# Output product with the weights as the stationary operand, and earlier due times behind the first top-k passes

## The chip, the cores and the metric

The kernel runs on one core of one Trainium2 chip. The metric is the device time of one execution in microseconds (us); the median of three runs of the kernel before is 1257.34 us (1255.83 to 1258.74). The engines are named as the profile names them: PE (TensorE matmuls), PEld (TensorE weight loads), DVE (VectorE), ACT (ScalarE), POOL (GpSimd), SP (the queue that issues the DMAs).

## What is computed

Attention that keeps the 32 largest scores of each row, then a gated feed-forward layer, then a second layer with a cosine. All in float32; 4 batches of 576 rows make 2304 tokens, 8 heads of 64 make 512 columns.

```python
scores = scale * np.matmul(q, k.transpose(0, 1, 3, 2))
kth = np.partition(scores, -top_k, axis=-1)[..., -top_k:-top_k + 1]
scores = np.where(scores >= kth, scores, -1000000000.0)
...
x = attention output as (2304, 512)
g = x @ w_gate
x = (silu(g) * (x @ w_val)) @ w_out      # 512 -> 1536 -> 512
h = x @ w_in                             # 512 -> 2048
out = (h * np.cos(h)) @ w_out2           # 2048 -> 512
```

## The kernel before

The 2304 tokens are 18 blocks of 128. `SIZES` puts them into ten chunks: two chunks of one block (c = 0 and 1, `TURNED`, c < `PLAIN`) and eight chunks of two blocks (c = 2 to 9). A chunk goes through four kinds of work.

**Attention** (`unit_proc`, `pair_proc`, `av_proc`, `x_proc`). A unit is one block and one head; there are 144. For each, PE makes the scores (L586 for c < 3, L593 later), ACT copies them out (L598), DVE runs four MAX8 (L623) and three MATCH_REPLACE8 (L626), and what follows the top-k passes is: POOL makes the bounds (L637, L641), ACT masks and exponentiates (L654, L665), PE transposes (L687) with ACT copying (L693), PE multiplies with V (L743), and POOL and ACT scale the rows by the sums (L754 to L824). For c < 2 the result is written by L807, later by L820 and L824.

**Gate and value product** (`turned_gemm_proc`, L989, for c < 2; `gemm_proc`, L899, later). For c >= 2 all operands are split into a high and a low part, so one product is three matmuls: high by high, high by low, low by high. There the weights are the stationary operand, 128 x 128, and 256 tokens move past them. The result G has the hidden columns in partitions and the tokens in the free dimension.

**Output product** (`wout_proc`, L1063; then `y_proc`). For each of the 12 groups f of 128 hidden columns and each of the two token blocks t, the stationary operand is the 128 x 128 slice of G and the 512 columns of the weights WO move: three matmuls of 512 columns. Each block has a PSUM bank of its own (`yt`, two banks). The sum stands with tokens in partitions, and the second layer needs it the other way round, so `y_proc` copies half a bank to SBUF (L1096, ACT), transposes it back into the bank in two 128 x 128 pieces (L1102, PE), copies it out again (L1107, ACT) and stores it to `y1` in DRAM (L1108, SP). The SBUF buffer `yo` is a single one (`r_yo = Ring(1)`), so the next half waits for the store.

**Second layer** (`h_proc`, L1279; `o_proc`, L1344), from some 850 us on; it reads `y1` back.

**Weight conversions.** The weights come in as 64-bit views and are brought into their form by `convert` (POOL L239 and L244, ACT L241 and L242) and split into high and low part (`w1_rest`, ACT L290, POOL and DVE L294). WO is loaded per chunk and f by `wo_proc` into two buffers.

**What sets the order.** Every step of work is yielded to a planner (`Plan`) with an engine, an estimated cost and a due time. The planner runs a model of the engines when the program is built: an engine that becomes free takes, of the steps that are ready in the model, the one that is due first. That fixes the order of the instructions in each engine's queue; on the chip an engine works through its queue in order. A unit's due time is 4.97 us times its number; what follows the top-k passes is due 0 to 15 us after it. The first conversions are due from -2.6 us on at steps of 3.1 us. `moe_due` gives the due times of a chunk's products.

Of the kernel before, what the change touches and what calls it, by code (L numbers as in the profile page):

```python
# [23 lines left out]
NTOK = B * S  # L24
# [137 lines left out]
def topk_attention_moe_moe(ctx: ExitStack, tc: tile.TileContext, qT, kT, vP, w1, wo1, w2, out):  # L162
# [53 lines left out]
    def due_unit(u):  # L216
        return u * PACE


# [346 lines left out]
    def unit_proc(u):  # L566
# [71 lines left out]

        end = yield "POOL", 0.175, bounds, due, True
        r_m.free(u, end, plan)  # L640
# [14 lines left out]

        end = yield "ACT", 0.68, keep, due + 6.0, True
        if h == 0:
# [9 lines left out]

        end = yield "ACT", 0.77, expo, due + 9.0, True
        ev_exp[u].set(end, plan)
# [4 lines left out]
    def group_proc(c, p, t, g, pt, made, done):  # L674
        u = unit_of[c, p, t, 1]
        due = due_unit(u) + 11.0 + g
        j0, j1 = GROUPS[g]
# [43 lines left out]
    def av_proc(c, p, g):  # L721
# [23 lines left out]

        due = due_unit(unit_of[c, p, t0 + n - 1, 1]) + 15.0
        end = yield "PE", 0.34 * len(segs) + 1.13 * n, attv, due, True
# [12 lines left out]
    def x_proc(c, p, g):  # L760
        t0, n = ATT[c][g]
        key = c, p, g
        due = due_unit(unit_of[c, p, t0 + n - 1, 1]) + 12.0
        yield ev_sum[key]
# [81 lines left out]
    GV0 = [sum(NF1 // 4 if turned else NF1 for turned in TURNED[:c]) for c in range(NCH)]  # L846
    ev_y1 = [Event() for _ in range(NTOK // 128)]
# [200 lines left out]

    def wout_proc(c):
        turned = TURNED[c]  # L1050
        for f in range(NF1):
            k = c * NF1 + f
            yield ev_g[c, f]
            yield ev_wo[c, f]

            def part(t, f=f, k=k):
                bank = yt[(FIRST[c] + t) % NYB]
                cs = slice(t * 128, t * 128 + 128)
                g = G[c, f // 2][:, f % 2] if turned else None
                terms = ((g, WO[k]),) if turned else [(G[c, f][m][:, cs], WO[k][:, a])  # L1060
                                                      for m, a in ((0, 0), (1, 0), (0, 1))]
                for n, (m, w) in enumerate(terms):
                    nc.tensor.matmul(bank, m, w, start=f == 0 and n == 0, stop=f == NF1 - 1 and n == len(terms) - 1)  # L1063

            for t in range(SIZES[c]):
                i = FIRST[c] + t
                if f == 0:
                    yield r_y[i % NYB].gate(i // NYB)
                end = yield "PE", 0.93 if turned else 0.7, lambda t=t, part=part: part(t), moe_due(c, f) + 5.0, False
                if f == NF1 - 1:  # L1070
                    plan.start(y_proc(c, i), end)
            if not turned:
                r_g.free(G0[c] + f, end, plan)
            elif f % 2 and f // 2 >= NG0:
# [5 lines left out]
        if turned:  # L1080
            r_x.free(2 + c, end, plan)

    def y_proc(c, i):
        due = moe_due(c, NF1)
        bank = yt[i % NYB]
        y4 = bank.rearrange("p (f n) -> p f n", f=KT)
        for half in range(2):
            ko = yo_count[0]
            yo_count[0] += 1
            yield r_yo.gate(ko)  # L1090
            y2 = y4[:, 2 * half:2 * half + 2]
# [14 lines left out]
            def store(y2=y2, half=half):  # L1106
                nc.scalar.activation(st["y"], y2, AF.Copy)  # L1107
                nc.sync.dma_start(y1[:, 2 * half:2 * half + 2, i * 128:i * 128 + 128], st["y"])  # L1108

            end = yield "ACT", 0.27, store, due, True  # L1110
            r_yo.free(ko, end + 2.5, plan)
        r_y[i % NYB].free(i // NYB, end, plan)
        ev_y1[i].set(end + 2.5, plan)

# [104 lines left out]
    def x2_proc(j):  # L1219
        yield ev_pb  # L1220
        pb = pools["pb"]
        for i in range(j * TPB, (j + 1) * TPB):
            yield ev_y1[i]
        due = b_due(j, 0) - (25.0 if j else 75.0)
# [23 lines left out]
    def h_proc(j, f):  # L1248
# [11 lines left out]
        if second:  # L1260
            yield r_y[i % 2].gate(NTOK // 128 // NYB)
        elif not third:
            yield ev_ph
# [128 lines left out]
    for c in range(NCH):  # L1392
        for f in range(NF1):
            if c:
                plan.start(wo_proc(c, f))
            if not TURNED[c]:
                plan.start(gemm_proc(c, f))
            elif f % 2:
                plan.start(turned_gemm_proc(c, f // 2))
        plan.start(wout_proc(c))  # L1400
    plan.start(pool_b_proc())
# [50 lines left out]
```

## Time and profile before

| | us |
|---|---|
| median of three runs | 1257.34 |
| the profiled execution | 1255.94 |
| its span, from the first instruction to the last | 1253.9 |
| PE busy in the span | 1200.3 (96%) |
| PEld busy | 1043.6 (83%) |
| DVE busy | 975.1 (78%) |
| ACT busy | 923.8 (74%) |
| POOL busy | 632.0 (50%) |

The page gives one execution. The span leaves 2.0 us of that execution's time outside, and the profiled execution is 1.4 us below the median. A share of the whole span is an average over the first layer with its attention and the second layer, so it has to be read stretch by stretch.

### The profile page before, as it was taken

The page shows a single profiled execution, that of the slowest core. Times are in us where ns is not written, and L with a number is a line of the kernel's source. Part 1 is how long each engine was busy: PE and PEld are TensorE (multiplying, and loading weights), DVE is VectorE, ACT ScalarE, POOL GpSimd, SP SyncE. Part 2 cuts the span into 40 slices and gives each one's busy share as a digit, 9 for nine tenths or more (in the row PEclk, how much of TensorE's full clock was granted, in tenths as well). Part 3 has the DMA queues.
Part 4 walks back from the last instruction along what each step waited for, and adds up shares of the span by engine and source line. Part 5 has one row for each costly group of instructions (what it writes and reads, how often), then busy time and mean ns, then how long its engine had stood idle before and what let it go on. Part 6 is the DMA issues. An engine that isn't in the chain of part 4 may idle for free.

```text
span 1253.9 us, 22487 instructions
## 1 busy us (share of the span) xinstructions
PE 1200.3 (96%) x7528; PEld 1043.6 (83%) x7528; DVE 975.1 (78%) x1938; ACT 923.8 (74%) x2081; POOL 632.0 (50%) x1082
## 2 busy tenths in 40 slices
PE   6799889999999999999999999999999999999998
PEld 3577657898888898988898988897999989898997
DVE  6999999999999999998999993447555555555553
ACT  4789999899888888888898876557565656565554
POOL 4898976776777776877776755533010101010000
PEclk9799989999999999999999999999999999999999
DMA  7555556665656655556555332871010101010000
GB/s 253 159 175 168 179 163 201 206 211 168 194 164 180 190 170 175 181 162 203 181 160 189 124 116 85 268 261 39 1 51 1 51 1 51 1 38 1 18 8 26
DMA packets 88547, 162.14 MB, mean 129 GB/s; under 512 B 17008, under 2 KB 44144, under 8 KB 88432
## 3 DMA queue, kind: packets, MB, share of 16 engines
q1 hardware_dynamic: 88272, 160.65, 40.4%
q8 instruction: 59, 0.97, 0.3%
q14 instruction: 56, 0.46, 0.1%
q10 hardware_dynamic: 160, 0.07, 0.0%
HBM read 133.41 MB, written 27.26 MB: 128 GB/s over the span
## 4 chain that ended last, share of the span: by engine, by line
PE 58%; DMA 8%; ACT 6%; POOL 3%; DVE 2%; issue 2%; SPq 0%; POOLq 0%; ACTq 0%
PE o L1344 16%; PE h L1279 15%; PE gv L899 10%; PE y L1063 7%; PE av L743 2%; PE sc L593 2%; DMA wo<-wo 2%; DMA kx<-in_kT 2%; PE tp L687 2%; PE gvl L899 2%; DMA y<-yo 1%; DMA w_raw<-in_w 1%; DMA qx<-in_qT 1%; ACT e L654 1%; POOL K L496 1%
## 5 line engine op out<-in xcount | busy, mean ns | idle before, releaser
L623 DVE MAX8 m<-w 128x8 f32<-128x576 f32 x432 | 311.0, 747 | 1.8
L899 PE MATMUL gv<-x,w 128*128 128x256 f32 x2016 | 283.7, 288 | 1.7 <-ACT hg L866 1.6
L899 PEld LDWEIGHTS gv<-x,w 128*128 128x128 f32 x2016 | 259.0, 190 | 8.6 <-ACT hg L866 2.8
L1279 PE MATMUL h<-x2h,w 128*128 128x384 f32 x768 | 214.5, 338 | 0.0
L626 DVE MATCH_REPLACE8 w<-m,w 128x576 f32<-128x576 f32 x288 | 213.3, 742 | 0.0
L1344 PE MATMUL o<-w,gh 128*128 128x512 f32 x576 | 195.8, 395 | 0.0
L1242 POOL TENSOR_TENSOR x2l<-x,x2h 128x384 fp32r<-128x384 f32 x24 | 25.8, 1075 | 262.1 <-ACT x2h L1231 262.1
L1063 PE MATMUL y<-wo,gh 128*128 128x512 f32 x400 | 148.5, 413 | 6.7 <-DMA wo<-wo 5.1
L1313 DVE TENSOR_TENSOR g<-r,h 128x384 f32<-128x384 f32 x96 | 53.1, 554 | 118.5 <-ACT r L1308 118.5
L1279 PEld LDWEIGHTS h<-x2h,w 128*128 128x128 f32 x768 | 140.6, 188 | 4.3
L1279 PE MATMUL h<-x2l,w 128*128 128x384 f32 x384 | 129.3, 337 | 0.0
L1306 ACT ACTIVATE r<-r 128x384 f32<-128x384 f32 x96 | 50.4, 525 | 103.9 <-DVE r L1303 103.9
L1344 PEld LDWEIGHTS o<-w,gh 128*128 128x128 f32 x576 | 108.1, 188 | 21.0
L654 ACT ACTIVATE e<-s,b 128x576 f32<-128x576 f32 x144 | 114.2, 794 | 8.2 <-POOL b L637 8.1
L623 DVE MAX8 m<-s 128x8 f32<-128x576 f32 x144 | 107.7, 748 | 15.9 <-ACT s L598 14.5
L665 ACT ACTIVATE e<-e,b 128x576 f32<-128x576 f32 x144 | 114.2, 793 | 2.8 <-POOL b L641 0.3
L1344 PE MATMUL o<-w,gl 128*128 128x512 f32 x288 | 113.6, 394 | 1.0 <-DVE gl L1327 1.0
L598 ACT ACTIVATE s<-sc 128x576 f32<-128x576 f32 x144 | 95.4, 662 | 21.6 <-PE sc L586 16.2
L626 DVE MATCH_REPLACE8 w<-m,s 128x576 f32<-128x576 f32 x144 | 106.9, 742 | 0.0
L693 ACT ACTIVATE pt<-tp 128x512 f32<-128x512 f32 (+1 forms) x216 | 101.9, 503 | 4.9 <-PE tp L687 3.3
L687 PE MATMUL tp<-ident,e 128*128 128x128 f32 x648 | 99.4, 277 | 5.9 <-ACT pt L693 3.3
L1327 DVE TENSOR_TENSOR gl<-g,gh 128x384 fp32r<-128x384 f32 x96 | 56.4, 588 | 58.0 <-ACT gh L1324 58.0
(106 smaller groups left out, 2489.6 us busy)
## 6 DMA issues: line engine op xcount, KB each, us to landing
wo<-wo SPq DMA_DIRECT2D x96, 512.0 KB, 3.7
w_raw<-in_w SPq DMA_DIRECT2D x32, 511.8 KB, 4.3
V<-in_vP SPq DMA_DIRECT2D x52, 256.0 KB, 3.0
w<-in_w SPq DMA_DIRECT2D x24, 511.5 KB, 5.5
kx<-in_kT SPq DMA_DIRECT2D x64, 144.0 KB, 3.1
wo<-wo SPq DMA_DIRECT2D x36, 256.0 KB, 2.9
w2d<-w_raw SPq DMA_DIRECT2D x32, 256.0 KB, 2.6
cvx<-w2d SPq DMA_DIRECT2D x32, 256.0 KB, 4.5
```

The source lines that it names most:

```text
L598: nc.scalar.activation(st["s"], sc[:, :, :HALF], AF.Copy)
L623: nc.vector.max(out=st["m"][:, 8 * i:8 * i + 8], in_=st["w"] if i else st["s"])
L626: nc.vector.match_replace(out=st["w"], in_to_replace=st["m"][:, 8 * i:8 * i + 8], in_values=st["w"] if i else st["s"], imm_value=LOWEST)
L654: nc.scalar.activation(st["e"], st["s"], AF.Prelu, bias=st["b"][:, 1:2], scale=SCALE, alpha=STEEP)
L665: nc.scalar.activation(st["e"], st["e"], AF.Exp, bias=st["b"][:, 2:3], scale=1.0, accum_out=smT[c, p, g][:, j:j + 1])
L687: nc.tensor.transpose(st["ps"][:, j - j0], e[:, j * 128:j * 128 + 128], ident)
L693: nc.scalar.activation(pt[:, j0:j1], st["ps"][:, :j1 - j0], AF.Copy)
L899: nc.tensor.matmul(gv[g], W1[f, kk // 2][:, a, g, kk % 2], m, start=kk == 0 and i == 0, stop=kk == KT - 1 and i == 2)
L1063: nc.tensor.matmul(bank, m, w, start=f == 0 and n == 0, stop=f == NF1 - 1 and n == len(terms) - 1)
L1279: nc.tensor.matmul(st["h"], w[:, a, kk * 128:kk * 128 + 128], m[:, kk], start=kk == 0 and n == 0, stop=kk == KT - 1 and n == 2)
L1327: end = yield "DVE", 0.46, lambda: nc.vector.tensor_sub(GT[j, f][1], st["g"], GT[j, f][0]), due, True
L1344: nc.tensor.matmul(o[t], a[:, cs], W2[f, 1][:, m], start=f == 0 and n == 0, stop=f == NF2 - 1 and n == 2)
```

## The change

For c >= 2 the output product takes WO as the stationary operand and lets the 256 tokens of G move. The sum then comes out with the 512 output columns in partitions, in four pieces d of 128 columns by 256 tokens, two pieces to a bank, and needs no transposing: a piece is copied out by one ACT instruction and stored. Chunks 0 and 1 keep the old form, as `turned_wout_proc`. For chunk 8 (`late`) the four copies go to four buffers of their own in the pool that opens when attention has ended. Beside that, for c < 2, the due times of what follows the top-k passes are 12 us earlier (`soon`), and the planned cost of a score step changes from 0.98 to 1.25 us for c < 3 and from 0.575 to 0.58 later.

```diff
+    y1p = [x.rearrange("p (a b) -> p a b", a=2) for x in yt]
+    def soon(c):
+        return 12.0 if c < PLAIN else 0.0
-        end = yield "PE", 0.575 * len(segs) if c >= RAWC else 0.98, qk, due - SC_LEAD, True
+        end = yield "PE", 0.58 * len(segs) if c >= RAWC else 1.25, qk, due - SC_LEAD, True
-        end = yield "POOL", 0.175, bounds, due, True
+        end = yield "POOL", 0.175, bounds, due - soon(c), True
-        end = yield "ACT", 0.68, keep, due + 6.0, True
+        end = yield "ACT", 0.68, keep, due + 6.0 - soon(c), True
-        end = yield "ACT", 0.77, expo, due + 9.0, True
+        end = yield "ACT", 0.77, expo, due + 9.0 - soon(c), True
...
+    def wout_proc(c):
+        t0 = FIRST[c] * 128
+        for f in range(NF1):
+            k = c * NF1 + f
+            due = moe_due(c, f) + 5.0
+            yield ev_g[c, f]
+            yield ev_wo[c, f]
+
+            def part(d, f=f, k=k):
+                w = WO[k]
+                gh, gl = G[c, f]
+                for i, (a, m) in enumerate(((0, gh), (0, gl), (1, gh))):
+                    nc.tensor.matmul(y1p[d // 2][:, d % 2], w[:, a, d * 128:d * 128 + 128], m,
+                                     start=f == 0 and i == 0 and d % 2 == 0, stop=f == NF1 - 1 and i == 2,
+                                     skip_group_check=True)
+
+            for d in range(KT):
+                if f == 0 and d % 2 == 0:
+                    yield r_y[d // 2].gate(bank_turn(c, d // 2))
+                end = yield "PE", 0.38, lambda d=d, part=part: part(d), due, False
+            r_g.free(G0[c] + f, end, plan)
+            r_wo.free(wo_index(c, f), end, plan)
+        due = moe_due(c, NF1)
+        late = c == NCH - 2
+        if late:
+            yield ev_pb
+        for d in range(KT):
+            if not late:
+                yield r_yo.gate(yo_count[0])
+
+            def fetch(d=d):
+                if late:
+                    y = pools["pb"].tile([128, CH], F32, tag=f"yo{d}", name="yo")
+                else:
+                    y = moe.tile([128, CH], F32, tag="yo", name="yo", bufs=r_yo.n)
+                nc.scalar.activation(y, y1p[d // 2][:, d % 2], AF.Copy)
+                nc.sync.dma_start(y1[:, d, t0:t0 + CH], y)
+
+            end = yield "ACT", 0.27, fetch, due, d == 0
...
+            if d % 2:
+                r_y[d // 2].free(bank_turn(c, d // 2), end, plan)
+        ev_y1[c].set(end + 2.5, plan)
```

The due times of the transposes and copies (`group_proc`), of the product with V (`av_proc`) and of the scaling (`x_proc`) get `- soon(c)` in the same way. `bank_turn` counts the turns of the two banks, and `ev_y1` is now one event per chunk.

## Rows read from the trace of the kernel before

**Rows 1.** Busy us of each engine by stretch, count, then clock, DMA share, GB/s

```profile
60.00:150.00 90.00, 85.77 (x470) 65.33 (x470) 87.28 (x183) 82.43 (x189) 81.57 (x133) 1.00 0.57 179
150.00:205.00 55.00, 45.85 (x225) 28.51 (x224) 51.83 (x103) 49.69 (x111) 37.43 (x55) 0.94 0.58 170
205.00:400.00 195.00, 189.97 (x1442) 169.12 (x1441) 191.59 (x399) 173.41 (x422) 145.69 (x261) 1.00 0.59 186
400.00:785.00 385.00, 379.20 (x2844) 339.10 (x2843) 349.99 (x717) 323.11 (x790) 268.95 (x505) 1.00 0.52 163
785.00:870.00 85.00, 79.41 (x509) 72.47 (x509) 46.89 (x72) 50.36 (x110) 41.83 (x35) 1.00 0.63 205
870.00:1254.00 384.00, 380.31 (x1900) 342.91 (x1898) 197.68 (x359) 208.60 (x393) 17.35 (x16) 1.00 0.06 21
```

**Rows 2.** Timelines around 763 to 786 us: start, length, engine, line, operation

```profile
762.21 0.76 DVE L623 MAX8 m<-w 128x8 f32<-128x576 f32 x1
784.46 0.74 POOL L824 TENSOR_TENSOR x<-rs,x 128x256 fp32r<-128x256 f32 x1 [0.53 <-ACT x L820]
785.91 5.20 PE L899 MATMUL gvl<-x,w 128*128 128x256 f32 x42
```

**Rows 3.** Timelines around 64 to 66 us and 201 us

```profile
64.24 0.26 ACT L754 ACTIVATE rx<-av 128x128 f32<-128x128 f32 x1
65.72 0.46 POOL L807 TENSOR_TENSOR xw<-rx,rs 128x128 f32<-128x128 f32 x1
201.71 0.73 POOL L824 TENSOR_TENSOR x<-rs,x 128x256 fp32r<-128x256 f32 x1 [0.36 <-ACT x L820]
201.90 1.31 PE L899 MATMUL gv<-x,w 128*128 128x256 f32 x9
```

**Rows 4.** Pieces of the chain that ended last: start, length, what

```profile
248.76 2.15 PE gv L899 x18
368.09 1.58 PE y L1063 x6
376.81 1.39 PE y L1063 x6
480.74 0.36 PE gv L899 x3
481.09 0.22 PE y L1102 x2
482.58 2.09 PE y L1063 x9
805.13 0.39 PE y L1102 x2
```

**Rows 5.** Groups by line and shape: count, busy us, mean ns, idle before

```profile
L899 PEld LDWEIGHTS gv<-x,w 128*128 128x128 f32 x2016 | 259.0, 190 | 8.6 <-ACT hg L866 2.8 <-issue 1.5
L1102 PE MATMUL y<-ident,yo 128*128 128x128 f32 x72 | 15.0, 290 | 3.2 <-ACT yo L1096 2.9
L1107 ACT ACTIVATE yo<-y 128x256 f32<-128x256 f32 x36 | 14.8, 412 | 2.4 <-PE y L1102 2.3
```

**Rows 6.** Waits of PE from 205 to 785 us: total us, times, longest

```profile
PE y L1102 <- ACT yo L1096: 1.7, 3, 1.0
PE y L1063 <- ACT yo L1107: 0.6, 1, 0.6
```

**Rows 7.** Waits of PE from 785 to 870 us

```profile
PE y L1063 <- DMA wo<-wo: 2.1, 2, 1.7
PE y L1102 <- ACT yo L1096: 1.1, 2, 0.6
```

**Rows 8.** Timeline of ACT where one chunk's sum is moved out

```profile
294.08 0.38 ACT L1096 ACTIVATE yo<-y 128x256 f32<-128x256 f32 x1
310.91 0.54 ACT L1107 ACTIVATE yo<-y 128x256 f32<-128x256 f32 x1
```

**Rows 9.** DMA issues by tile: count, KB each, median us to landing

```profile
y<-yo SPq DMA_DIRECT2D x36, 128.0 KB, 2.0
```

More of the change, by code (lines that the diff above doesn't have):

```diff
@@ L846, in topk_attention_moe_moe @@
     GV0 = [sum(NF1 // 4 if turned else NF1 for turned in TURNED[:c]) for c in range(NCH)]
[L847 removed]
+    ev_y1 = [Event() for _ in range(NCH)]
     yo_count = [0]
@@ L1047, in turned_gemm_proc, with bank_turn, turned_wout_proc, part @@
             ev_g[c, 2 * fp + j].set(end, plan)
-    def wout_proc(c):
-        turned = TURNED[c]
+    def bank_turn(c, b):
+        return c // 2 if c < PLAIN else c - PLAIN + (PLAIN + 1 - b) // 2
+    def turned_wout_proc(c):
+        bank, b = yt[c % NYB], c % NYB
+        yield r_y[b].gate(bank_turn(c, b))
         for f in range(NF1):
-            k = c * NF1 + f
             yield ev_g[c, f]
             yield ev_wo[c, f]
[L1056 to L1074, printed above, removed]
+            def part(f=f):
+                nc.tensor.matmul(bank, G[c, f // 2][:, f % 2], WO[c * NF1 + f], start=f == 0, stop=f == NF1 - 1)
+            end = yield "PE", 0.93, part, moe_due(c, f) + 5.0, False
+            if f % 2 and f // 2 >= NG0:
                 r_g.free(G0[c] + (f // 2 - NG0) // 2, end, plan)
@@ L1079, in wout_proc @@
                 wo0_free(f, end)
-        if turned:
-            r_x.free(2 + c, end, plan)
-    def y_proc(c, i):
+        r_x.free(2 + c, end, plan)
         due = moe_due(c, NF1)
-        bank = yt[i % NYB]
         y4 = bank.rearrange("p (f n) -> p f n", f=KT)
         for half in range(2):
-            ko = yo_count[0]
-            yo_count[0] += 1
-            yield r_yo.gate(ko)
+            yield r_yo.gate(yo_count[0])
             y2 = y4[:, 2 * half:2 * half + 2]
@@ L1107, in store @@
                 nc.scalar.activation(st["y"], y2, AF.Copy)
-                nc.sync.dma_start(y1[:, 2 * half:2 * half + 2, i * 128:i * 128 + 128], st["y"])
+                nc.sync.dma_start(y1[:, 2 * half:2 * half + 2, FIRST[c] * 128:FIRST[c] * 128 + 128], st["y"])
             end = yield "ACT", 0.27, store, due, True
-            r_yo.free(ko, end + 2.5, plan)
-        r_y[i % NYB].free(i // NYB, end, plan)
-        ev_y1[i].set(end + 2.5, plan)
+            r_yo.free(yo_count[0], end + 2.5, plan)
@@ new lines, in turned_wout_proc @@
+            yo_count[0] += 1
+        r_y[b].free(bank_turn(c, b), end, plan)
+        ev_y1[c].set(end + 2.5, plan)
[25 more added lines that the diff above has]
+            if not late:
+                yield r_yo.gate(yo_count[0])
+            def fetch(d=d):
[6 more added lines that the diff above has]
+            end = yield "ACT", 0.27, fetch, due, d == 0
+            if not late:
+                r_yo.free(yo_count[0], end + 2.5, plan)
+                yo_count[0] += 1
+            if d % 2:
+                r_y[d // 2].free(bank_turn(c, d // 2), end, plan)
+        ev_y1[c].set(end + 2.5, plan)
@@ L1221, in x2_proc @@
         pb = pools["pb"]
-        for i in range(j * TPB, (j + 1) * TPB):
-            yield ev_y1[i]
+        for c in range(NCH):
+            if FIRST[c] < (j + 1) * TPB and FIRST[c] + SIZES[c] > j * TPB:
+                yield ev_y1[c]
         due = b_due(j, 0) - (25.0 if j else 75.0)
@@ L1399, in topk_attention_moe_moe @@
                 plan.start(turned_gemm_proc(c, f // 2))
-        plan.start(wout_proc(c))
+        plan.start((turned_wout_proc if TURNED[c] else wout_proc)(c))
     plan.start(pool_b_proc())
```

8 lines of the change are left out of this document (4 added, 4 removed).

## The prediction

> **What bounds the kernel now.** I read the busy time by stretches first, since the page's shares mix two layers. The columns are PE, PEld, DVE, ACT and POOL, then the granted clock and the DMA. From 870 us on PE is busy 380.3 of 384 us and nothing of the change lies there [rows 1]: that stretch only moves as a whole. So the question is when it begins. From 205 to 785 us two engines are nearly full at once, PE with 569.2 of 580 us and DVE with 541.6 [rows 1]. Which of the two sets the end is seen where attention ends: the last MAX8 of the last top-k ends at 763.0 us, the last piece of attention is written at 785.2 us, and the product of the last chunk follows within a microsecond, at 785.9 us, without a gap on PE [rows 2]. So for 22.2 us after DVE was done PE still had work queued, with no gap before chunk 9: a backlog, and a microsecond less on PE after about 200 us is a microsecond less at 785 us until it is gone. How large it is no row says. The gate and value products of chunks 2 to 8 are 2016 matmuls [rows 5] of 0.119 us [rows 4], 241 us, the output products of seven chunks 84 x 1.39 us [rows 4], 117 us: together 358 of the 580 us, or 62%. If the 22.2 us are like the rest, some 14 us of them are products, and that is the room, as an estimate.
>
> The other end of the backlog is the start of chunk 2's product, at 201.9 us, just as the last piece of that chunk's attention is being written (201.7 us) [rows 3]. Between 150 and 205 us PE is idle 9.2 us, while DVE is busy 51.8 of 55 us and was busy 87.3 of 90 us before [rows 1]. There the top-k passes set the pace, and PE's idle time costs nothing.
>
> So the sum is: what PE has to do, and waits for, after 202 us; and by how much the start at 201.9 us moves.
>
> **The change, part by part.**
>
> *The matmuls.* There are 8 chunks x 12 f = 96 groups. Each was 6 matmuls of 512 columns and is 12 of 256, with the same number of columns. A run of nine of 512 took 2.09 us, 232 ns each; a run of 18 of 256 with weights in the same form took 2.15 us, 119.4 ns each [rows 4]. Per group 12 x 0.1194 = 1.433 us against 6 x 0.232 = 1.393 us: 0.040 us more, and 96 x 0.040 = **+3.8 us**.
>
> The Trainium skill speaks against this part: "Larger matmuls are more efficient than smaller matmuls, when possible" (Perfetto Trace Analysis, Optimizing Tensor Performance, Matmuls). The rows agree in sign, 119.4 against 116.1 ns for 256 columns. By the fixed 2.5 ns that a warm matmul costs in TensorE: Matmul & The Clock Gate, section Back-to-back issue gap, 576 further matmuls would be an estimated 1.4 us in place of 3.8.
>
> *Finer steps.* A group was two steps of 0.7 us and becomes four of 0.36 us (three matmuls of 256 took 0.36 us [rows 4]). The planner may put other work between any two steps, and a run of six that follows other work took 1.58 us where another took 1.39 us [rows 4]: 0.19 us for a break. Bounds: no further break, 0; one further break in every group, 96 x 0.19 = 18 us. The four steps have one due time, as the two had, so only work that becomes ready in the middle gets between. I take one group in ten: **+1.8 us**, near the lower end because six in one run is the pattern that the chain shows.
>
> *The transposes back.* 72 are recorded [rows 5]; 8 belong to chunks 0 and 1 and stay, 64 go, in 32 pairs. A pair lengthened the chain by 0.22 us, in the worst row by 0.39 us [rows 4]: 7.0 to 12.5 us. I take the lower, which is the unhindered one: **-7.0 us**. Their waits go too: PE waited for the first copy 1.7 us up to 785 us and 1.1 us after, and 0.6 us for the second copy before it could use a bank again [rows 6, 7]: **-3.4 us**.
>
> *The moving out.* A chunk had four uses of the single `yo` buffer, each copy, transposes, copy, store; from the first copy to the end of the last took 294.1 to 311.5 us, 17.4 us [rows 8]. It stays at four uses, each one copy and one store. The store lands in 2.0 us [rows 9], a copy takes 0.4 us [rows 5], so four uses take about 10 us, and the next chunk finds its banks earlier. ACT loses 32 instructions of 0.41 us [rows 5], 13 us by record, beside work that ends later; I count nothing. The new wait is that a copy stands at the head of ACT's queue until the last store has landed, and behind it stand the copies that feed PE and DVE. The plan allows 2.5 us for the landing, above the 2.0 us of the row, so I take 0; if each of three such waits in seven chunks were 0.5 us over, ACT would lose 10 us, less than the 13 us that it gains. On SP the number of stores stays 32 and each still waits for an ACT copy, with the loads of K, Q and WO queued behind it; it comes sooner by a pair of transposes.
>
> *Chunk 8 and 9.* With four buffers chunk 8's copies run without waiting for stores, so chunk 9's output product may begin some 10 us earlier, and its weights, loaded into two buffers, are asked for earlier. PE waited 2.1 us for these loads after 785 us [rows 7]. Bounds 0 and -2.1; the DMA engines are at 0.63 there [rows 1], with a denser part, so I take half: **-1.0 us**.
>
> *Earlier due times in chunks 0 and 1, dearer score steps in the plan.* No work is added or removed; in ACT's and POOL's queues the attention steps move ahead of conversions (L239 to L242, L290, L294), and on PE they move ahead of L989. Chunk 0's last piece was written at 65.7 us after a copy at 64.2 us [rows 3]; that can come some 3 us sooner, and the conversions that it overtakes come later by the same sum, with weights of later f not yet needed. But what counts is the start at 201.9 us, and before it DVE is full [rows 1]. What can be gained is that conversions are out of the way of chunk 2's last steps. If all of DVE's idle time between 60 and 205 us were recovered that is 5.9 us [rows 1]; if the overtaken conversions collide with chunk 2 instead, each that stands in the way costs about what a POOL piece costs, 0.7 us [rows 3], and four of them some 3 us. I take **-1.5 us** between -5.9 and +3, since DVE leaves little.
>
> Sum: 3.8 + 1.8 - 7.0 - 3.4 - 1.0 - 1.5 = -7.3 us. The profiled execution of before took 1255.94 us, so 1248.6 us; it was 1.4 us under the median, so 1250.0 us as a median. Next to be late, once PE is 7 us shorter, is attention itself: some 14 us of room were estimated above, so the gain is not cut, but twice of it would be.
>
> **The rivals.**
>
> *PE is not what decides (same).* If DVE and the chain behind it set 785 us after all, the saving in chunks 2 to 7 is returned as idle time on PE, and only what chunks 8 and 9 save after 763 us is left: two of eight chunks of (3.8 + 1.8 - 7.0 - 3.4) = -4.8 us, that is -1.2 us, and -1.0 us of weight waits: 1255 us. For it speaks that DVE is busy 191.6 of 195 us from 205 to 400 us; against it that it is 35 us idle from 400 to 785 us [rows 1]. The case in which the due times change hardly any order and the plan's finer steps eat half the gain lands there too.
>
> *The steps are broken up (slower).* Mechanism: with steps of 0.36 us on PE, transposes and score steps slip between them, each break at 0.19 us [rows 4]. The other terms give -9.1 us, so it decides from 48 of 96 groups broken once more; with all broken 18.2 - 9.1 = +9 us, 1266 us; with two in three broken +3 us, 1260 us. For it: PE's queue has something due nearly always. Against: equal due times.
>
> *Weight loads set PE's pace (slower).* The change adds 576 loads at 190 ns [rows 5], 109 us, where PEld already has 508 of 580 us [rows 1]. If loads could not overlap, the stretch would end some 37 us later, at 1294 us. Against it stands the run of 18 in 2.15 us [rows 4]: 18 loads of 190 ns are 3.4 us and yet ran in 2.15. The Trainium skill (Perfetto Trace Analysis, Identifying the Most-Contended Engine) wants PE's headroom judged by this busy share; the run of 18 shows that the records overlap, so that 100% is no limit here.
>
> *More than the sum (faster).* The early order and the sooner banks close PE's gaps too: 10.8 us idle from 205 to 785 us and 5.6 us after [rows 1]. Half of that on top gives 1242 us.
>
> **How the numbers follow.** Forecast (-3 to -11 us, 1246 to 1254): 0.51. More than the sum: 0.13. PE not deciding: 0.19. Broken steps or colliding conversions: 0.15. Weight loads: 0.02. About 0.2%, 2.5 us, is what a measurement can tell from no change. Faster takes the forecast and the larger gain, 0.64; same 0.19; slower 0.17. The range reaches from the larger gain to a small loss, 1242 to 1259 us; half of the larger-gain case lies under it and two thirds of the slower ones over it, together under a fifth.
>
> **What would show it.** Right: no L1102 for chunks 2 to 9 (8 left); the new L1063 form at about 0.12 us a matmul in runs of 12; the product of the last chunk starting 5 to 7 us earlier than 785.9 us, with the same 384 us behind 870 us moved as a whole. Wrong: L1063 mostly in runs of three; PE idle between 205 and 785 us grown from 10.8 us; ACT waiting for y stores; chunk 2's product starting later than 201.9 us.

## The result, and the profile after

The changed kernel took **1266.08 us** (median; 1263.0 to 1268.91) beside 1256.59 us for the kernel before: a ratio of 1.0084, with a 95% interval from 1.006 to 1.0108. It is slower by some 10 us, where 1250.0 us had been predicted, and it lies above the range. The ratio is not the quotient of the two medians, which would be 1.0076, or 9.5 us; where a difference below is given "by the ratios", it is taken from such ratios, otherwise from the medians. Its profiled execution took 1265.69 us, with a span of 1263.9 us.

The kernel after by stretches, with the columns and stretches of [rows 1] from 150 us on:

```profile
150.00:205.00 55.00, 45.55 (x236) 29.41 (x234) 52.34 (x102) 49.17 (x110) 35.79 (x56) 0.97 0.56 169
205.00:400.00 195.00, 186.77 (x1550) 173.24 (x1550) 189.31 (x389) 169.06 (x405) 144.44 (x256) 1.00 0.57 183
400.00:785.00 385.00, 374.07 (x3114) 350.68 (x3113) 355.46 (x726) 320.94 (x775) 266.97 (x504) 1.00 0.50 162
785.00:870.00 85.00, 78.37 (x588) 75.79 (x587) 40.30 (x61) 44.75 (x97) 45.55 (x40) 0.96 0.64 215
870.00:1254.00 384.00, 384.00 (x1923) 347.08 (x1922) 202.73 (x368) 211.43 (x400) 17.08 (x16) 1.00 0.06 20
```

PE is idle 8.2 + 10.9 = 19.2 us from 205 to 785 us, where it had been 10.8. Between 785 and 870 us it is idle 6.6 us, and the granted clock there is 0.96 instead of 1.00. Three rows of the timeline of PE and DVE answer to [rows 2] (start, length, engine, line, operation):

```profile
770.12 0.76 DVE L627 MAX8 m<-w 128x8 f32<-128x576 f32 x1
793.94 1.24 PE L903 MATMUL gvl<-x,w 128*128 128x256 f32 x9
864.65 0.39 PE L1379 MATMUL o<-w,gh 128*128 128x512 f32 x1
```

The last MAX8 stands 7.9 us later than before and the product of the last chunk starts 8.0 us later (785.91 before). The first output product of layer 2 starts at 864.65 us, where the timeline of before has it at 853.35: 11.3 us later.

The work itself changed as foreseen. Pieces of the chain, and groups by line and shape, of the kernel after (answering to [rows 4] and [rows 5]):

```profile
331.25 1.44 PE y L1115 x12
365.39 1.44 PE y L1115 x12
```

```profile
L1115 PE MATMUL y<-gh,wo 128*128 128x256 f32 x768 | 158.7, 288 | 9.2 <-DMA wo<-wo 4.2 <-ACT e L658 1.7 <-ACT gh L962 1.7
L1089 PE MATMUL y<-ident,yo 128*128 128x128 f32 x8 | 1.7, 293 | 2.5 <-ACT yo L1083 2.5
L1138 ACT ACTIVATE yo<-y 128x256 f32<-128x256 f32 x32 | 12.3, 392 | 2.7 <-DMA y<-yo 1.6 <-PE y L1115 0.9
```

A group of 12 matmuls takes 1.44 us, 8 transposes are left, and the moving out is 32 copies which waited 1.6 us in all for their buffer's store. From 205 to 785 us PE was busy 560.8 us instead of 569.2, and over the whole span 1200.2 us against 1200.3: hardly less work by record, and it took longer.

### The profile page after: what moved, and what is told of

The parts are those of the page before. It is cut to its first block, busy times and chain, and to the rows that moved or that the text cites. A ratio compares the mean times of both kernels' runs of the same rounds, so it can differ in the third digit from the quotient of the medians.

```text
span 1263.9 us, 23394 instructions
## 1 busy us (share of the span) xinstructions
PE 1200.2 (95%) x8040; PEld 1070.7 (85%) x8040; DVE 980.2 (78%) x1938; ACT 917.5 (73%) x2049; POOL 631.7 (50%) x1082
## 4 chain that ended last, share of the span: by engine, by line
PE 52%; DVE 13%; ACT 11%; POOL 10%; DMA 9%; issue 4%; SPq 1%; POOLq 0%; ACTq 0%; DVEq 0%
PE o L1379 16%; PE h L1314 16%; DVE m L627 6%; DVE w L630 6%; PE gv L903 6%; PE y L1115 5%; PE gvl L903 2%; DMA w_raw<-in_w 2%; DMA qx<-in_qT 2%; DMA wo<-wo 2%; PE tp L691 2%; PE av L747 2%; PE sc L597 2%; POOL K L500 2%; ACT e L669 1%
## 5 line engine op out<-in xcount | busy, mean ns | idle before, releaser
L903 PEld LDWEIGHTS gv<-x,w 128*128 128x128 f32 x2016 | 255.2, 191 | 8.5 <-ACT hg L870 5.3
L1115 PE MATMUL y<-gh,wo 128*128 128x256 f32 x768 | 158.7, 288 | 9.2 <-DMA wo<-wo 4.2
L1115 PEld LDWEIGHTS y<-gh,wo 128*128 128x128 f32 x768 | 126.7, 191 | 16.9 <-issue 5.6
L1115 PE MATMUL y<-gl,wo 128*128 128x256 f32 x384 | 110.9, 289 | 4.6 <-POOL gl L966 2.7
```

Of the source, the lines that this page charges most:

```text
L903: nc.tensor.matmul(gv[g], W1[f, kk // 2][:, a, g, kk % 2], m, start=kk == 0 and i == 0, stop=kk == KT - 1 and i == 2)
L1115: nc.tensor.matmul(y1p[d // 2][:, d % 2], w[:, a, d * 128:d * 128 + 128], m, start=f == 0 and i == 0 and d % 2 == 0, stop=f == NF1 - 1 and ...
```

## The experiments

Several kernels leave work out, so that only their times count: `pe_less` and `before_pe_less` skip the product with the low half of the gate (`gl`) in the output product of chunks 2 to 9; `dve_less` skips one replacement pass in every third top-k; `before_both_less` skips both. All ratios are to the kernel before, run beside the kernel on the same chip (its medians there: 1254.1 to 1254.9 us); 0.001 is 1.25 us.

### The two halves of the change, each alone

**wout_only** is the changed kernel without the early due times and the dearer score step.

```diff
-        return 12.0 if c < PLAIN else 0.0
+        return 0.0
...
-        end = yield "PE", 0.58 * len(segs) if c >= RAWC else 1.25, qk, due - SC_LEAD, True
+        end = yield "PE", 0.575 * len(segs) if c >= RAWC else 0.98, qk, due - SC_LEAD, True
```

> The new output product alone: due times and planned score costs as before. Theory A (the new form of the product costs the time, by its finer steps or by where it puts the copies and stores): 1264 to 1268 us. Theory B (the earlier due times and the dearer planned score step cost it): 1255 us or less, and 1250 if the prediction's other terms hold.

Measured: 1260.33 us, ratio 1.0049 [1.0033, 1.0065].

**plan_only** is the kernel before with only those two.

```diff
+    def soon(c):
+        return 12.0 if c < PLAIN else 0.0
...
-        end = yield "PE", 0.575 * len(segs) if c >= RAWC else 0.98, qk, due - SC_LEAD, True
+        end = yield "PE", 0.58 * len(segs) if c >= RAWC else 1.25, qk, due - SC_LEAD, True
...
-        end = yield "POOL", 0.175, bounds, due, True
+        end = yield "POOL", 0.175, bounds, due - soon(c), True
...
```

> The kernel before with only the earlier due times of chunks 0 and 1 and the new planned costs of the score steps. Theory A (the product costs the time): 1253 to 1258 us. Theory B (these cost it): 1264 us or more.

Measured: 1256.51 us, ratio 1.0027 [1.0008, 1.0046]. Neither half gains anything. The product alone lies between the two times expected; the due times and costs alone lie in the range of theory A, but by the ratio they cost some time too. Together they would make 1.0076, and the change has 1.0084, which the intervals can't tell from a sum.

Where the saving went can be read between the start of chunk 2's product and that of the last chunk, here for before, wout_only and plan_only in this order (columns as in [rows 1]):

```profile
201.90:785.91 584.01, 572.73 (x4311) 511.59 (x4308) 544.68 (x1122) 499.94 (x1218) 416.02 (x768) 1.00 0.54 171
201.20:786.33 585.13, 571.52 (x4761) 535.08 (x4760) 547.61 (x1122) 495.36 (x1194) 416.27 (x766) 1.00 0.54 170
198.54:787.25 588.71, 573.37 (x4324) 513.48 (x4322) 546.68 (x1125) 503.62 (x1223) 417.71 (x768) 1.00 0.55 171
```

In wout_only PE works 1.2 us less, which is what the prediction's terms for matmuls, finer steps and transposes make for seven of eight chunks, but it is idle 13.6 us instead of 11.3, where 2.3 us less had been expected. In plan_only the product of chunk 2 starts 3.4 us sooner, PE is idle 15.3 us, and the last chunk's product starts 1.3 us later. These are single executions.

### Does PE set the pace in layer 1?

The prediction counted a microsecond off PE as a microsecond. Four kernels cut PE, DVE or both, with the order of everything else kept.

**pe_less**, on the changed kernel, has 46 us less on PE:

```diff
-                for i, (a, m) in enumerate(((0, gh), (0, gl), (1, gh))):
+                for i, (a, m) in ((0, (0, gh)), (2, (1, gh))):
```

> The kernel after, with the same planned order, but the matmul of the low part of G (256 columns) left out of every step of the new output product: 384 matmuls of 0.12 us, 46 us less on PE. If PE sets the pace from 205 us on, as predicted: some 1220 us. If the top-k passes on DVE set it: only what PE saves after the last top-k counts, some 15 groups of 0.48 us, so 1257 to 1261 us.

Measured: 1257.82 us, ratio 1.0032 [1.0015, 1.0049]. By the ratios that is 6.5 us less than the changed kernel, for 46 us of work.

**dve_less**, on the changed kernel, has 32 us less on DVE (behind the MAX8 of pass i of unit u):

```diff
+                if i == 1 and u % 3 == 0:
+                    return
```

> The kernel after, with the same planned order, but one of the three MATCH_REPLACE8 left out in every third unit: 48 of 0.66 us, 32 us less on DVE. If DVE sets the pace: 20 us less or more, up to what PE's idle time allows, 1240 to 1246 us. If PE sets it: 1262 to 1266 us.

Measured: 1263.81 us, ratio 1.0065 [1.0045, 1.0085]: 2.4 us less by the ratios, with intervals that overlap. So `pe_less` lies where it was expected if DVE sets the pace, and `dve_less` where it was expected if PE does: neither engine does so alone.

**before_pe_less** makes the cut on PE, 44.5 us, in the kernel before, on which the prediction was read:

```diff
                 for n, (m, w) in enumerate(terms):
+                    if n == 1:
+                        continue
```

> The kernel before, same planned order, the matmul of the low part of G left out of the output product of chunks 2 to 9: 192 matmuls of 0.232 us, 44.5 us less on PE. If PE sets the pace of the kernel before, as the prediction read it: some 1215 us. If another engine or the order of the queues does: 1246 to 1252 us, little more than what is saved after the last top-k.

Measured: 1246.11 us, ratio 0.9917 [0.9887, 0.9948]: 8.6 us less (10.4 by the ratio). So even here some four fifths of a cut on PE come to nothing. In its profile the last top-k unit starts 5.6 us sooner than before and the last chunk's product 8.8 us sooner (777.09 us), although some 33 us of the cut lie in chunks 2 to 7; the rest of the cut shortens the way from there to the end by 1.6 us. Where the rest went is in two stretches of its profile (columns as in [rows 1]):

```profile
205.00:485.00 280.00, 263.22 (x2027) 232.22 (x2026) 275.51 (x579) 251.23 (x614) 210.44 (x385) 1.00 0.59 187
485.00:765.00 280.00, 263.82 (x1996) 232.98 (x1995) 262.40 (x533) 235.57 (x579) 195.51 (x368) 1.00 0.52 161
```

and in the chain of work from 205 to 765 us, whose shares by engine and line are, in the kernel before and then in before_pe_less:

```profile
by line: PE gv L899 21.1%; PE y L1063 11.7%; PE sc L593 5.3%; DMA kx<-in_kT 5.0%; PE av L743 5.0%; PE tp L687 4.6%; issue 3.9%; DMA wo<-wo 3.3%; DMA w_raw<-in_w 2.3%; DMA qx<-in_qT 1.9%; ACT e L654 1.8%; POOL K L496 1.8%; DMA w2d<-w_raw 1.8
by line: DVE m L623 26.3%; DVE w L626 24.0%; issue 5.7%; PE gv L899 4.7%; DMA qx<-in_qT 2.3%; ACT e L654 2.1%; DMA w2d<-w_raw 2.1%; ACT e L665 2.0%; POOL K L496 1.8%; DMA w_raw<-in_w 1.7%; POOL w_raw L244 1.5%; ACT pt L693 1.4%; PE av L743 
```

PE is idle 33 of 560 us, three times what it was in 580 us of the kernel before, and the chain, which ran through PE for about half of its length, now runs for half of its length through DVE's passes (26.3 and 24.0%): the top-k stood right behind PE. What remained was to cut both.

**before_both_less** is both cuts on the kernel before.

> The kernel before, same planned order, with both cuts: the low-part matmuls of the output product left out (44.5 us of PE) and one MATCH_REPLACE8 left out in every third unit (32 us of DVE). If PE and DVE are both at their limit and each hides a cut in the other: 25 us less or more, under 1230 us. If what sets the pace is a third engine or the waits between queues in the planned order: within 5 us of the run with the PE cut alone.

Measured: 1241.36 us, ratio 0.9875 [0.9842, 0.9907]: 13.3 us less for 76 us of work (15.7 by the ratio), 4.8 us more than the cut on PE alone (5.3 by the ratios). That is at the edge of the 5 us that were set for a third engine or the order, and far from the 25 us of two full engines. Its two stretches:

```profile
205.00:485.00 280.00, 266.28 (x2049) 236.10 (x2048) 266.27 (x546) 253.27 (x620) 212.42 (x388) 0.99 0.60 189
485.00:765.00 280.00, 266.44 (x2028) 237.42 (x2028) 247.77 (x494) 237.99 (x584) 198.42 (x373) 1.00 0.51 161
```

No engine is full: PE 95%, DVE 92%, ACT 88%. The chain has no line over 15% any more (gate product 14.4%, output product 5.5%, score, transposes, copies and loads 2 to 5% each). The reading that fits is that engines whose queues follow one planned order wait for each other in turn, so that taking work from one or two of them shortens little. It is argued and not shown: which further engine or load would have to be cut too wasn't tried.

### The two halves together: a stall at 510 us

The starts of the top-k units (144 in all), read from the timeline of DVE, show where the changed kernel falls behind: against before it is 2.9 us late at unit 96 (508 us), 8.5 us at unit 104 (550 us), and 7.9 us at the last one. In wout_only unit 104 is 0.5 us late. A piece of the chain of the changed kernel in that place, and its waits from 505 to 565 us (total us, times, longest):

```profile
513.48 1.28 POOL w_raw L248
514.77 0.02 issue
514.78 3.40 DMA w2d<-w_raw
518.18 0.02 issue
518.20 6.79 DMA w_raw<-in_w
```

```profile
ACT c L245 <- DMA w_raw<-in_w: 3.9, 2, 3.2
PE tp L691 <- ACT pt L697: 3.5, 2, 3.0
DVE m L627 <- ACT s L602: 3.4, 2, 3.1
```

A raw weight block of layer 2 is loaded into a buffer that a store must leave first; the load is planned at 2.1 us and took 6.8. The conversion that needs it stands at the head of ACT's queue, and behind it the score copy for DVE and the copies for PE wait 3 us. In the kernel before the same conversion waits 1.1 us at the longest in this stretch. Behind the load the chain runs on from 526 to 545 us mostly through POOL, so the load need not be all of the stall. In dve_less, which keeps the changed kernel's order, it recurs (unit 96 late by 1.5 us, unit 104 by 7.4, ACT waiting 2.1 us at the longest for `w_raw`); in pe_less, with that order too, ACT has no such wait there.

**after_old_cost** is the changed kernel with the old planned cost of the score step, **after_no_soon** the one with the old due times (the second and the first of the two edits of wout_only, each alone).

> The kernel after with the old planned costs of the score steps; product and earlier due times as in after. If the parts add up and the planned cost is the part that costs: 1260 us. If the earlier due times cost: 1266. If the rest of the loss is an accident of the order that all three parts together give: 1260 without a stall of several us around 520 us.

> The kernel after without the earlier due times; product and new planned costs as in after. If the earlier due times are the part that costs: 1260 us. If the planned costs: 1266. If it is an accident of the order: 1260 without the stall around 520 us.

Measured: 1262.47 us, ratio 1.0052 [1.0035, 1.0069], last unit 0.4 us sooner than before, no stall; and 1263.06 us, ratio 1.0064 [1.0043, 1.0085], unit 104 late by 2.4 us and unit 128 by 5.0. Both lie between the 1260 and the 1266 us that were expected, so neither edit by itself is the part that costs.

**after_raw5** leaves the change whole and only plans that load longer.

```diff
-        yield "DMA", 2.1, load, due - 8.0, True
+        yield "DMA", 5.0, load, due - 8.0, True
```

> The changed kernel, and the load of the second layer's raw weights during attention is planned at 5.0 us in place of 2.1. In the changed kernel unit 104 starts 8.5 us later than before, of which some 5 us arise between 510 and 558 us, where the chain goes through a store of such weights (3.4 us) and their load (6.8 us) and ACT stands for that load with a conversion at the head of its queue, score copies behind it. Theory, queue: with the longer planned load the conversions stand further back, the jump is gone, unit 104 is at most 4.5 us later than before, and the time falls by 3 to 5 us: 1260 to 1263. Rival: the jump is not those conversions (the longer planned score product has the whole order too slow from 205 us on); then unit 104 stays 7 us late or more and the time within 1.5 us of 1265.

Measured: 1258.42 us, ratio 1.0046 [1.0026, 1.0066]. Unit 104 is 1.8 us late instead of 8.5, no wait of ACT for `w_raw` stands among those from 505 to 565 us, and the kernel is where the new product alone is. By the ratios the gain is 4.8 us, at the upper end of what was expected (the median is below the 1260 to 1263 us that were given). No work differs, so this loss, 1.0084 to 1.0046, is one of order, and what was foretold of unit 104 and of ACT's wait points to the conversion that waits for a load. It isn't proved to be that alone: the intervals just overlap, and the edit changes the order in the queues from some 194 us on.

### The seam of the two layers

In wout_only attention ends with before (last unit 0.4 us sooner, product of the last chunk from 786.3 us on), and it still loses. What follows is best read from two points on PE's timeline: the end of the last matmul of the last chunk's gate product (`gvl`), and the end of the span.

| kernel | form in chunks 8, 9 | last gvl ends, after gvl's start | from there to the span's end |
|---|---|---|---|
| before | old | 58.6 | 409.4 |
| plan_only | old | 59.6 | 409.4 |
| before_x2_later | old | 58.2 | 409.0 |
| wout_last_old | old | 58.4 | 409.4 |
| before_last_new | new | 61.5 | 411.3 |
| wout_only | new | 59.5 | 411.9 |
| after | new | 58.5 | 411.5 |
| wout_no_late | new | 59.7 | 411.2 |
| wout_x2_later | new | 60.4 | 409.5 |
| wout_last2 | new | 58.5 | 409.8 |
| after_raw5_x2_later | new | 61.4 | 409.5 |

In most of these kernels the new form loses some 2 us behind the last gate matmul, although it has fewer matmuls there (no transposes, one group instead of two). PE's waits of wout_only in that place, from its timeline, and its stretches (columns as in [rows 1]):

```profile
849.28 0.39 PE L1115 MATMUL y<-gh,wo 128*128 128x256 f32 x1 [0.88 <-ACT gh L962]
851.22 0.58 PE L1115 MATMUL y<-gl,wo 128*128 128x256 f32 x1 [1.55 <-DVE gl L966]
860.23 0.45 PE L1314 MATMUL h<-x2h,w 128*128 128x384 f32 x1 [1.83 <-DVE g L1348]
```

```profile
840.00:850.00 10.00, 8.79 (x63) 8.27 (x62) 4.58 (x8) 7.49 (x14) 5.64 (x5) 1.00 0.53 171
850.00:855.00 5.00, 3.79 (x17) 3.79 (x18) 5.00 (x4) 4.14 (x10) 5.00 (x4) 0.66 0.23 79
855.00:860.00 5.00, 3.40 (x17) 2.66 (x15) 5.00 (x7) 3.14 (x8) 5.00 (x4) 1.00 0.08 26
860.00:865.00 5.00, 4.77 (x17) 4.43 (x18) 3.55 (x8) 3.64 (x9) 0.11 (x1) 0.66 0.08 26
```

PE stands 0.88 and 1.55 us with a single matmul between, and then the granted clock falls from 1.00 (2.4 GHz) for a part of the next 5 us (1.2 GHz); the group's other eleven matmuls run from 851.22 to 853.73 us, 2.5 us for what takes 1.3. After the next wait, 1.83 us, it falls again. At 0.66 two stretches of 5 us cost at most (1 - 0.66) x 10 = 3.4 us of work, an estimate for a PE that is busy throughout. The kernel before has waits of 1.48 and 0.97 us in this place, with 4 us of work between them, and its clock stays at 1.00 (the two waits, then two stretches):

```profile
849.75 0.50 PE L1063 MATMUL y<-wo,gl 128*128 128x512 f32 x1 [1.48 <-DVE gl L962]
854.72 0.49 PE L1344 MATMUL o<-w,gl 128*128 128x512 f32 x1 [0.97 <-DVE gl L1327]
845.00:850.00 5.00, 3.52 (x17) 2.82 (x17) 4.39 (x6) 5.00 (x11) 3.56 (x3) 1.00 0.22 76
850.00:855.00 5.00, 4.03 (x21) 3.37 (x21) 5.00 (x4) 4.21 (x10) 5.00 (x4) 1.00 0.09 26
```

The Trainium skill (TensorE: Matmul & The Clock Gate, Part 1) says that the clock follows how busy PE has been recently. These rows agree in part: each fall stands behind waits of PE, but not every such wait has a fall behind it.

**wout_last_old** is wout_only with the old form, transposes and all, in chunks 8 and 9; **before_last_new** is the kernel before with the new form in these two alone.

```diff
-        plan.start((turned_wout_proc if TURNED[c] else wout_proc)(c))
+        plan.start((turned_wout_proc if TURNED[c] else wout_proc if c < NCH - 2 else old_wout_proc)(c))
```

```diff
-        plan.start(wout_proc(c))
+        plan.start((new_wout_proc if c >= NCH - 2 else wout_proc)(c))
```

> The new output product alone (old due times, old planned score cost), but chunks 8 and 9 keep the old form with its transposes; up to 786 us the order is that of the new product alone. The kernel before took 1254.1 us beside the last runs, the new product alone 1260.3. Theory, tail: the saving in chunks 2 to 7 comes back as idle time and the loss is made in chunks 8 and 9, so with their old form the time is that of before, 1252 to 1255.5 us. Rival, everywhere: six of eight chunks keep the new form and with it most of the loss, 1258 to 1260.

> The kernel before, but chunks 8 and 9 have the new form with its four buffers for chunk 8. Theory, tail: two chunks of new form cost what all eight did, 1258 to 1260.5 us, with the granted clock under 1.00 for some 3 us between 785 and 870 us, where before shows none. Rival, everywhere: a quarter of the loss, 1255 to 1256; by the prediction's own terms (two of eight chunks and the weights sooner) it would be 1252.

Measured: 1256.59 us, ratio 1.0010 [0.9994, 1.0027], between the two ranges expected; and 1259.11 us, ratio 1.0035 [1.0016, 1.0054], where the theory had it, with the clock at 0.88, 0.50 and 0.94 in the three stretches of 5 us from 850 us on. Six chunks of the new form, which by the prediction's terms save some 3 us, lie between a gain of 0.8 and a loss of 3.4 us; two at the end cost most of the loss.

**wout_no_late** is wout_only with chunk 8's copies through the single buffer.

```diff
-        late = c == NCH - 2
+        late = False
```

> The new output product alone (old due times, old planned score cost), but chunk 8's four copies go through the single buffer as those of the chunks before do, so each waits until the store of the one before has landed, and chunk 9 finds its second bank some 6 us later. The kernel before takes 1254.1 to 1254.9 us, the new product alone 1260.3. Theory, four buffers: with them chunk 9's groups run too early, catch up with the gate that feeds them, and PE stands for the last gh and gl copies (0.9 and 1.55 us) with the clock falling behind it; four stores at 793 to 796 us stand ahead of weight loads on SP. Without them the first hidden product of layer 2 comes near 806 us again (811.8 now), the clock is 1.00 from 840 to 870 us, and the time is 1254 to 1256.5. Rival, the form itself: without transposes to fill gaps PE still arrives early at the last group; clock under 1.00 again, and the time 1259 to 1261.

Measured: 1259.52 us, ratio 1.0035 [1.0020, 1.0050]; the clock falls to 0.66 from 860 to 865 us. By the ratios that is 1.8 us less than with the four buffers, with intervals that overlap; the rival holds, they are not what costs most.

**wout_x2_later** and **before_x2_later** hold back the second layer's loads of x for token block 1 and later, which stand between the last weight loads, and whose copies on ACT wait for them ahead of the last gate copy.

```diff
         yield r_x2s.gate(j)
+        if j:
+            yield ev_h[j - 1, 4]
```

> The new output product alone (old due times, old planned score cost), and in the second layer the loads of x for token block 1 and later (four per block, with their ACT copies x2h) may only be placed once the fifth hidden product of the block before is done; up to 828 us nothing moves. The kernel before took 1254.2 us beside it, the new product alone 1260.3. Theory, clock and queue: in the new product alone three such loads stand among the last weight loads of layer 1 (828.9, 840.6 and 843.7 us), ACT's copies of them stand at the head of its queue for 2.5, 1.35 and 1.5 us, the last gate copy that feeds the last output group comes late (848.8 us), PE is idle 0.9 and 1.55 us and then 1.8 us, and the granted clock falls to 0.66 in 850 to 855 and in 860 to 865 us, 3.4 us of work. Without them the clock stays at 1.00 there and the time falls by 3 to 5 us, to 1255 to 1257. Rival: the loss after 786 us is only that PE no longer has products to fill its waits with; then the clock still falls and the time stays within 1.5 us of 1260.

> The same placement of the second layer's x loads on the kernel before, which shows a clock of 1.00 from 785 to 870 us. Theory, clock and queue: at most the 1.2 us that ACT stood for x loads after 834 us and the 1.5 us wait before the last output group come back: 1252.5 to 1254.5 against 1254.2. If the loads cost every order alike (rival), it gains the same 3 to 5 us as the new product does, 1249 to 1251.

Measured: 1257.30 us, ratio 1.0029 [1.0014, 1.0043]; and 1254.16 us, ratio 0.9998 [0.9982, 1.0015]. It gains 2.5 us by the ratios in the new order (the intervals overlap at their ends) and nothing in the old one, as the theory had it, though a little less than the 1255 to 1257 us expected, and the way from the last gate matmul to the end is 409.5 us. That the clock would stay at 1.00 held up to 860 us only: it is 0.83 from 860 to 870 us. Ahead of the last gate matmul this kernel takes 0.9 us longer than wout_only.

**after_raw5_x2_later** has both edits on the changed kernel.

> Both edits together on the changed kernel. If the two losses are apart, one at 510 to 558 us in attention and one at the seam of the layers, they add: 1256 to 1259 us, with 1.00 of clock from 850 to 870 us. If either edit only shuffles an order, the sum of the two single gains is missed by over 2 us.

Measured: 1256.26 us, ratio 1.0015 [1.0002, 1.0028]. That is in the range for two losses that lie apart and add up: 8.7 us by the ratios, where the single gains make 7.3. The clock of 1.00 from 850 to 870 us, which was expected too, did not come: it is 0.98 from 855 and 0.68 from 860 us.

**wout_last2** moves one group. In the program's order of before two output groups of chunk 9 stand behind the last gate matmul; in wout_only one does, and the other stands three matmuls ahead of it.

```diff
-            due = moe_due(c, f) + 5.0
+            due = moe_due(c, f) + (15.0 if c == NCH - 1 and f >= NF1 - 2 else 5.0)
```

> The new output product alone, and the due time of the last two output groups of chunk 9 is 10 us later, so that the last but one stands behind the last gate matmul on PE, as in the kernel before, and not three matmuls ahead of it. The kernel before takes 1254.8 us, the new product alone 1260.3. Theory, one group's place: the last gate product ends 58 us after its first matmul and not 59.5, its copies gh and gl come some 1.4 us sooner, and the group that now stands behind it covers PE's wait for them (0.9 and 1.55 us before); the clock is 1.00 from 845 to 858 us, and the time falls by 2 to 4 us, to 1256 to 1258.5. Rival: the hidden and output products of layer 2 then wait for the chain of elementwise work instead, the clock falls all the same, and the time stays within 1.5 us of 1260.

Measured: 1257.30 us, ratio 1.0028 [1.0013, 1.0043], in the range expected, though this interval too touches that of wout_only. The same waits in its timeline, and the stretches from 850 us:

```profile
846.72 0.38 PE L1115 MATMUL y<-gh,wo 128*128 128x256 f32 x1 [0.42 <-ACT gh L962]
848.66 0.38 PE L1115 MATMUL y<-gl,wo 128*128 128x256 f32 x1 [1.56 <-DVE gl L966]
857.71 0.45 PE L1314 MATMUL h<-x2h,w 128*128 128x384 f32 x1 [1.74 <-DVE g L1348]
```

```profile
850.00:855.00 5.00, 5.00 (x29) 4.79 (x29) 5.00 (x6) 2.95 (x7) 5.00 (x4) 1.00 0.16 52
855.00:860.00 5.00, 3.26 (x18) 2.73 (x17) 4.67 (x9) 4.56 (x10) 2.58 (x2) 1.00 0.12 32
860.00:865.00 5.00, 5.00 (x26) 4.47 (x25) 3.40 (x8) 3.84 (x8) 1.26 (x1) 1.00 0.44 136
```

The first wait is half as long, the others are as they were, and the clock stays at 1.00. From the last chunk's first gate matmul to the end it takes 468.3 us, against 471.4 in wout_only and 468.0 before. So 2.6 of the 6.1 us that the new product loses (by the ratios) go with the place of one group. How much of it is the clock isn't shown. This profile is the fastest of the kernel's twelve executions (1255.42 us); over all of them the median of the mean granted clock is 0.992, no higher than the 0.9925 of wout_only (before: 0.993), and after_raw5_x2_later goes from the last gate matmul to the end in 409.5 us with a clock that falls.

### How much is the order itself?

**before_pace498** and **wout_pace498** change the planned distance of the top-k units by 0.2%. No work changes, only the order in the queues.

```diff
-    PACE = 4.97
+    PACE = 4.98
```

> The kernel before with the plan's distance between top-k units, from which all due times of layer 1 follow, at 4.98 in place of 4.97: no work changes, only the order in the queues. If orders are alike, the time is within 1 us of before (1253 to 1255). If a shuffled order alone moves the time by as much as the whole change (9.5 us) did, a large part of the loss would be the order: then 1248 to 1262, and I expect a shift of 2 to 5 us, rather up than down, since the old order was chosen at 4.97.

> The new output product alone with the same 4.98. If the new form costs by itself, it stays 4 to 6 us over the kernel before at 4.98. If the loss is the luck of one order, the distance between the two changes by over 3 us, or its sign.

Measured: 1257.39 us, ratio 1.0022 [1.0004, 1.0040]; and 1260.27 us, ratio 1.0045 [1.0025, 1.0065]. A shuffled order alone costs the kernel before 2.5 us (an interval from 0.5 to 5). The new product stays above it, but by 2.9 us here instead of 6, with intervals that overlap. The distance changed by 3.3 us, over the 3 us that were set for the luck of one order: about half of the new product's loss may be the order, and at 4.98 it isn't shown to lose at all.

## Why the prediction was wrong, point by point

- **"A microsecond less on PE after about 200 us is a microsecond less at 785 us."** This step failed, and with it the sign. The 22.2 us between the last MAX8 and the last piece of attention [rows 2] were read as a backlog of PE with 14 us of room. With 44.5 us less on PE in that same kernel the way from the start of the last unit to the last chunk's product was still 26.0 us, against 29.2: it is mostly the length of the way itself. The product started 8.8 us sooner, the kernel gained 8.6 us, and DVE became half of the chain. The small saving of the change fared no better: in wout_only PE worked 1.2 us less up to that product and was idle 2.3 us more. An engine at 98% with another at 93% beside it [rows 1] has no room that can be read from its own busy time. The rival "PE is not what decides" had the mechanism (the saving comes back as idle time on PE: 19.2 us against 10.8) but took the remainder as a gain; it also named DVE as what decides, and with both cut only 13.3 of 76 us came back.
- **Matmuls, +3.8 us:** the price was right. 1.44 us for a run of 12 against 1.39 is 0.05 us a group, 4.8 us for the 96.
- **Finer steps, +1.8 us:** right. In the program's order of the changed kernel 82 runs are of 12 matmuls, 6 of 18, 9 of 6 and 2 of 3: of the 96 groups 88 are whole, 7 are broken once and one twice, where one in ten was assumed. The slower rival of broken steps reached the right time for a reason that did not occur.
- **Transposes, -7.0 us, and their waits, -3.4 us:** the work is gone and the microseconds are not, for the first reason. The waits hardly went: PE stood for the moving out 2.0 us from 205 to 785 us (1.5 in chunks 2 to 7, 0.5 for turned copies that stay), against 2.3 [rows 6].
- **Moving out, 0:** right. ACT waited 1.6 us for stores from 205 to 785 us; the waits of the kernel before have 2.1.
- **Chunk 8 and 9, -1.0 us between 0 and -2.1:** wrong in sign. Here the new form costs 4.3 us by itself (before_last_new, 1.0035; its interval reaches from 2.0 to 6.8 us). The term priced the loads and banks of chunk 9 and left out what the groups, once they come sooner, no longer cover: PE's wait for the last gate copies, behind which the clock fell. The wait for weights rose too, from 2.1 [rows 7] to 2.6 us.
- **Due times and planned score cost, -1.5 us between -5.9 and +3:** chunk 2's product did start sooner, at 199.72 us against 201.90 [rows 3], but the whole of it costs 3.4 us alone (1.0027; 2.4 by the medians). The start of chunk 2 is not what the end hangs on; what comes in the following 580 us is, where PE was idle 4.1 us more (plan_only). In the full change it also met the stall at 510 us.

What stays open: that the saving doesn't arrive is shown; why the kernel got slower is shown in part. Of the new product's loss some 3.5 us (wout_last2 is still at 1.0028) are not assigned to one place, the share of the clock at the seam isn't known, and 2.5 us is what an order without any change of work may cost, which is as much as several of the single steps above.

## What to carry to other kernels

Where queues run in order and several engines are nearly full, as here (PE 98%, DVE 93%, ACT 86% from 205 to 785 us), price a saving by what stands directly behind the engine, not by its own share; cut the work out for a test, and see how much comes back. At the seam of two phases look for the work that covers a wait, since a saving there can uncover it, and a PE that stands for two microseconds may pay again in its clock. Shift the order a little without changing the work, and see how far the time moves, before a few microseconds are given a cause. A step whose input is a load belongs in an in-order queue only behind the load's true landing time: where 2.1 us were planned and 6.8 passed, ACT, DVE and PE each waited some 3 us.

## What the hardware showed that was not expected

The clock fell behind waits of PE as short as 0.88 and 1.55 us with one matmul between, but not behind 0.42 and 1.56 us, nor 1.48 and 0.97; in the changed kernel it was 0.74 and 0.58 in two stretches of 5 us from 855 us on, behind 1.69 and 1.54 us. What makes the difference isn't shown. And one profile is no measure of a few microseconds: wout_only and wout_x2_later have the same order on every queue up to 828 us, yet the last chunk's product starts at 786.3 us in the one and 789.7 us in the other. The profile of wout_x2_later is the slowest of its ten executions.
